# The second product of the last two blocks as seven products of sums (Strassen), in a sigmoid attention and MLP kernel on Trainium2

## The chip, the core and the metric

The kernel runs on one core of one Trainium2 chip. The metric is the device time of one execution in microseconds. The engines named below are TensorE (PE; PEld is its weight load), VectorE (DVE), ScalarE (ACT) and SyncE (SP), which only issues DMAs. GpSimd does nothing here.

## The reference

Sigmoid attention over 8 batches, 12 heads, 448 positions and head size 64, then an MLP of 768 -> 2048 -> 768 over all 3584 tokens, in float32:

```python
scores = scale * np.matmul(q, k.transpose(0, 1, 3, 2)) - np.log(S)
attn = 1.0 / (1.0 + np.exp(-scores))
x = np.matmul(attn, v)          # then tokens x 768
h = x @ w_in
g = h * (1.0 / (1.0 + np.exp(-1.702 * h)))
out = g @ w_out
```

## The kernel before

**Precision.** TensorE multiplies float32r. Every factor of a product that has to be exact is split in two parts, the rounded value and the rest; a product of two such factors is three matmuls: high by low, low by high, high by high. `round_and_rest` (L354) makes the parts: a cast (L357 on ScalarE or L358 on VectorE, whichever the plan finds free) and a subtraction on VectorE (L363).

**Blocks.** The 3584 tokens are 7 blocks of 512. Weights are 32 tiles of 128 x 768: 16 for w_in (f = 0 to 15) and 16 for w_out. They come as float64, are decoded, stored as float32 (`whole`), split, and stored as parts (`halves`, 128 x 1536: the rounded part, then the rest). From then on a block loads its weights from `halves` into the buffers `wsplit`, of which there are 3. The five blocks of `mlp` (L904) do the first layer ("up", 16 columns of 18 matmuls) and the second ("down", 6 columns of 48 matmuls).

**Attention** of later batches runs between the products of the blocks. Its batches 3 to 7 are `packed_attention` (L832): 60 units, one for a head of a pair, each of some scores (L717), sigmoids (L723), splits (L673, L765, L772) and a product with v (L806). Results are added into the blocks' x (L821); for blocks 3 to 5 x goes to HBM and back (`xd`).

**Order.** All instructions are put in an order beforehand by `Plan` (L78). It plays the tasks through with estimated costs; TensorE takes main units in their sequence and attention units as they fall due, the other engines take the ready task with the earliest key. `BUFS` says how many buffers each tag has; a new use of a buffer depends on all users of the use that many before it. `on_either` (L342) leaves ScalarE or VectorE to the plan. On the chip every engine runs its list in order, waiting on semaphores. All DMAs are issued by SyncE, in one list, so a DMA whose data isn't ready holds up all that are behind it.

**The last two blocks** (`last_blocks`, L987) are taken as one. Their x is a matrix of 2 x 2 quarters: two halves of the 768 inputs by two blocks (`one`, `two`). For the first layer, `up(n)` (L1059, n = 0 to 7) takes a pair of weight columns f, f2 (`columns`, L855) as a 2 x 2 matrix as well and makes the four results by seven products (Strassen's method in Winograd's form) rather than eight, 9 matmuls each (L1085). The factors of x (a11, a12 from x; s1 to s4 and a22 in the 15 buffers `xs`) are made once, by VectorE, after the attention has ended. Of the weights' sums (`sums_of_weights`, L858), there is one for each of the 8 column pairs: two loads of `whole`, four subtractions (L871), two splits, two stores (`sums`). They are tied to units 20, 25, ... 55 of the packed attention (L841).

The results h go through the sigmoid (L1047), the product with h (L1050) and `round_and_rest`, which makes the parts of g (`activated`, L1041), in 16 buffers `g`.

The second layer of the last two blocks (`down`, L1133) is plain: after every four `up` it adds up one half of the 16 rows of weights for all 6 output columns and both blocks: 2 halves x 6 x 2 x 8 x 3 = 576 matmuls (L1176). The first half's sums go to HBM (`od`) and come back (`osum`) to be added to the second's (L1004). A loaded buffer of weights holds 6 weight blocks, each used for both blocks, 36 matmuls.

Of the kernel before, what the change touches and what calls it, by code (L numbers as in the profile page):

```python
# [9 lines left out]
F32 = mybir.dt.float32  # L10
F32R = mybir.dt.float32r
# [9 lines left out]
P = 128  # L21
# [3 lines left out]
T = 512  # L25
# [230 lines left out]
def sigmoid_attention_mlp(ctx: ExitStack, tc: tile.TileContext, qk, v, v2, w, out):  # L256
# [575 lines left out]
    def packed_attention():  # L832
        units, late, n = [], [], 0
        for b in range(PACKED, B):
            for p in range(NP):
                loaded = load_pair(b, p)
                for j in range(2):
                    one, two, three = head(b, p, j, loaded)
                    units.append(one + two + late)
                    late = three  # L840
                    if len(units) > 18 and len(units) % 5 == 0 and n < NF // 2:  # L841
                        sums_of_weights(n, two)
                        n += 1
        assert n == NF // 2
        return [*units, late]

# [5 lines left out]
            for n in range(NF // 2)]  # L852
    summed = {}

    def columns(n):  # L855
        return 8 * (n // 4) + n % 4, 8 * (n // 4) + n % 4 + 4

    def sums_of_weights(n, after):  # L858
# [7 lines left out]
        h0, h1 = slice(0, HW), slice(HW, 2 * HW)  # L866

        def less(i, a, b, deps, first=lambda: None):
            def emit():
                first()  # L870
                nc.vector.tensor_tensor(t.tile[:, i * HW : (i + 1) * HW], a(), b(), op=ALU.subtract)  # L871

            return task("DVE", 0.55, emit, deps, [t, wa, wb])

        def of(i):
            return lambda: t.tile[:, i * HW : (i + 1) * HW]

        t1 = less(0, lambda: wb.tile[:, h0], lambda: wa.tile[:, h0], loads,
                  lambda: make(t, "raw64", [P, 2 * NW_EL], F32, f"sums{n}"))
        t2 = less(1, lambda: wb.tile[:, h1], of(0), [t1])  # L880
        t3 = less(2, lambda: wb.tile[:, h1], lambda: wb.tile[:, h0], [t1])
        t4 = less(3, lambda: wa.tile[:, h1], of(1), [t2])
# [104 lines left out]
    def last_blocks():  # L987
# [19 lines left out]

        for i in range(NK // 2):
# [11 lines left out]
            in_parts("a22", i, lambda b=a22: b.tile, wrote[two, i + NK // 2], [a22])  # L1020
            t1 = combine(lambda b=s1: b.tile, lambda b=a21: b.tile, lambda b=a22: b.tile, ALU.add, ready,
                         [s1, a21, a22], lambda b=s1, i=i: make(b, "line", [P, T], F32, f"s1_{i}"))
            in_parts("s1", i, lambda b=s1: b.tile, [t1], [s1])
            t2 = combine(lambda b=s2: b.tile, lambda b=s1: b.tile, lambda b=a11: b.tile, ALU.subtract,
                         [t1, l11], [s2, s1, a11], lambda b=s2, i=i: make(b, "line", [P, T], F32, f"s2_{i}"))
            in_parts("s2", i, lambda b=s2: b.tile, [t2], [s2])
            t3 = combine(lambda b=a21: b.tile, lambda b=a11: b.tile, lambda b=a21: b.tile, ALU.subtract,
                         [t1, l11], [a21, a11])
            in_parts("s3", i, lambda b=a21: b.tile, [t3], [a21])
            t4 = combine(lambda b=a12: b.tile, lambda b=a12: b.tile, lambda b=s2: b.tile, ALU.subtract,  # L1030
                         [t2, l12], [a12, s2])
            in_parts("s4", i, lambda b=a12: b.tile, [t4], [a12])

        units, gs = [], {}

# [5 lines left out]
        def activated(block, f, h, t, uses):  # L1041

            g, gb = buffer("line"), buffer("g")

            def sigmoid():
                make(g, "line", [P, T], F32, f"g{block}_{f}")
                nc.scalar.activation(g.tile, h(), AF.Sigmoid, scale=1.702)  # L1047

            t = task("ACT", 0.6, sigmoid, [t], [g, *uses])
            t = task("DVE", 0.69, lambda: nc.vector.tensor_tensor(g.tile, h(), g.tile, op=ALU.mult),  # L1050
                     [t], [g, *uses])
            t = round_and_rest(
                (0.62, 0.42, 0.69), gb, lambda: g.tile, [t], [g],
                lambda: gb.tile[:, 0], lambda: gb.tile[:, 1],
                lambda: make(gb, "g", [P, 2, T], F32R, f"gs{block}_{f}"),
            )
            gs[block, f] = (t, gb)
# [73 lines left out]
        halved = {}  # L1131

        def down(half):  # L1133

            fs = [8 * half + f for f in range(8)]
            blocks = [m * NF + f for m in range(NM) for f in fs]
            loaded, at = [], {}
            for n in range(0, len(blocks), NK):
                b = buffer("wsplit")
                ts, c = [], 0  # L1140
                for src, run in itertools.groupby(blocks[n : n + NK], lambda x: x // NK):
                    run = list(run)
                    while run:
                        count = next((i for i in range(1, len(run)) if run[i] != run[0] + i), len(run))
                        k, c0 = run[0] % NK, c
                        ts.append(dma(
                            lambda b=b, c0=c0, count=count: b.tile.bitcast(F32).rearrange(
                                "p (t c) -> p t c", t=2)[:, :, c0 * P : (c0 + count) * P],
                            lambda src=src, k=k, count=count: halves[NF + src].rearrange(
                                "p (t c) -> p t c", t=2)[:, :, k * P : (k + count) * P],  # L1150
                            2 * KB * count / NK, [saved[NF + src]], [b],
                            lambda b=b, n=n: b.tile is None and make(
                                b, "wsplit", [P, 2 * NW_EL], F32R, f"wd{half}_{n}"),
                        ))
                        for i in range(count):
                            at[run[i]] = (b, c0 + i, ts[-1])
                        run, c = run[count:], c + count
            turns = [(0, 1), (2, 4), (5, 6), (3, 7)]
            for m in range(NM):
                groups = []  # L1160
                for j, block in enumerate((one, two)):
                    bank = "m" if j == 0 else ("m0", "av")[m % 2]
                    groups.append((block, bank, buffer(bank)))
                steps = [(turn, g) for turn in turns for g in groups]
                if half and m == NM - 1:
                    steps = [(turn, g) for g in groups for turn in turns]
                for turn, (block, bank, ps) in steps:
                    pairs = [(at[m * NF + fs[i]], gs[block, fs[i]]) for i in turn]

                    def emit(pairs=pairs, ps=ps, bank=bank, turn=turn, block=block, m=m):  # L1170
                        if ps.tile is None:
                            make(ps, bank, [P, 512], F32, f"o{block}_{m}_{half}")
                        for i, ((b, c, _), (_, gb)) in zip(turn, pairs):
                            ws = [b.tile[:, j * NW_EL + c * P : j * NW_EL + (c + 1) * P] for j in range(2)]
                            for j, (u, d) in enumerate(((0, 1), (1, 0), (0, 0))):
                                nc.tensor.matmul(  # L1176
                                    ps.tile, lhsT=ws[u], rhs=gb.tile[:, d],
                                    start=i == 0 and j == 0, stop=i == 7 and j == 2,
                                )

                    t = task("PE", 6 * 0.2267, emit,
                             [d for x, g in pairs for d in (x[2], g[0])],
                             [ps, *(x[0] for x, _ in pairs), *(g[1] for _, g in pairs)])
                    units.append([t])
                    if turn != turns[-1]:
                        continue
                    if half == 0:
                        o = buffer("line")
                        t = on_either(
                            (0.59, lambda o=o, ps=ps: nc.scalar.copy(o.tile, ps.tile)),  # L1190
                            (0.69, lambda o=o, ps=ps: nc.vector.tensor_copy(o.tile, ps.tile)),
                            [t], [o, ps],
                            lambda o=o, block=block, m=m: make(o, "line", [P, T], F32, f"half{block}_{m}"),
                        )
                        d = dram.tile([P, T], F32, name=f"od{block}_{m}", tag=f"od{block}_{m}")
                        halved[block, m] = d, dma(
                            lambda d=d: d, lambda o=o: o.tile, P * T * 4 / 1024, [t], [o])
                    else:
                        d, t_d = halved[block, m]
                        o = buffer("x32")  # L1200
                        t_o = dma(lambda o=o: o.tile, lambda d=d: d, P * T * 4 / 1024, [t_d], [o],
                                  lambda o=o, block=block, m=m: make(o, "x32", [P, T], F32, f"osum{block}_{m}"))
                        t = combine(lambda o=o: o.tile, lambda ps=ps: ps.tile, lambda o=o: o.tile, ALU.add,
                                    [t, t_o], [o, ps])
                        dma(lambda block=block, m=m: out[block, m], lambda o=o: o.tile,
                            P * T * 4 / 1024, [t], [o])
# [69 lines left out]
```

## Time and profile before

| what | value |
|---|---|
| median of 3 runs | 1193.51 us (1192.75 to 1194.01) |
| the profiled execution | 1193.79 us |
| its span, first to last instruction | 1191.9 us |
| granted TensorE clock | 1.00 |
| TensorE busy | 1185.0 us, 5517 matmuls |
| VectorE busy | 873.0 us |
| ScalarE busy | 718.5 us |
| last matmul of the attention | 917 us |
| first layer of the last two blocks | 943.2 to 1000.3 and 1065.6 to 1122.7 us |
| their second layer | 1000.3 to 1065.6 and 1122.7 to 1188.0 us |

A row of the groups reads: line, engine, operation, output <- inputs by the program's names, shapes, count | busy us, mean ns of one | idle time of the engine just before them and what ended it. A row of the stages reads: stretch, then for each engine its busy us and its count, then the clock, the share of the 16 DMA engines, and GB/s. A row of the chain or the timeline reads: start, length, engine, line, what, count.

### The profile page before, as it was taken

To read this page: it belongs to the slowest core of one execution; us is meant where nothing else is said; L and a number is where in the kernel's file an instruction comes from. 1 tells how busy PE (TensorE), PEld (TensorE's weight loads), DVE (VectorE), ACT (ScalarE), POOL (GpSimd) and SP (SyncE) were. 2 spreads that over 40 slices of the span, in tenths; PEclk is the share of its full clock that TensorE was granted. 3 is DMA by queue.
4 is the path that set the end of the run, shared out by engine and by line. 5 is a ranking of instruction groups with operands and counts; after the bars stand their busy time and mean duration, and the time that the engine had idled before them with its cause. 6 is when DMAs were issued, how large, how long until landed. Compare 5 with 4: busy or idle time off the path is not lost.

```text
span 1191.9 us, 15238 instructions
## 1 busy us (share of the span) xinstructions
PE 1185.0 (99%) x5517; PEld 955.2 (80%) x5517; DVE 873.0 (73%) x1443; ACT 718.5 (60%) x1127; POOL 0.2 (0%) x4
## 2 busy tenths in 40 slices
PE   9999999999999999999999999999999999999998
PEld 4457777788888888888888888888888888888887
DVE  6989998769998598998789998588896464006511
ACT  7898887466787577786577786477784233013300
POOL 0000000000000000000000000000000000000000
PEclk9999999999999999999999999999999999999999
DMA  9966568867777655867766677757565755446652
GB/s 345 312 194 230 186 223 291 263 222 281 265 268 244 242 189 193 293 209 292 260 231 240 219 283 249 270 193 270 198 242 189 258 189 168 148 159 211 204 194 79
DMA packets 82154, 274.08 MB, mean 230 GB/s; under 512 B 8640, under 2 KB 15808, under 8 KB 82080
## 3 DMA queue, kind: packets, MB, share of 16 engines
q1 hardware_dynamic: 82080, 273.12, 66.9%
q8 instruction: 43, 0.70, 0.2%
q14 instruction: 31, 0.25, 0.1%
HBM read 203.88 MB, written 69.21 MB: 229 GB/s over the span
## 4 chain that ended last, share of the span: by engine, by line
PE 96%; DMA 2%; DVE 1%; ACT 1%; issue 0%; SPq 0%; ACTq 0%
PE h L912 28%; PE o L912 25%; PE o L1176 11%; PE sc L717 7%; PE av L806 7%; PE m L1085 5%; PE av L557 5%; PE sc L534 4%; PE sc L1085 3%; PE av L1085 1%; DMA wsplit<-w 1%; DMA wsum<-f 1%; DMA qkraw<-qk 0%; ACT a L545 0%; DVE qk L673 0%; DVE alo L772 0%
## 5 line engine op out<-in xcount | busy, mean ns | idle before, releaser
L912 PE MATMUL o<-gs,wsplit 128*128 128x512 f32 x1440 | 334.2, 390 | 0.6 <-DMA wsplit<-w 0.5
L912 PE MATMUL h<-x,wsplit 128*128 128x512 f32 x1440 | 334.1, 390 | 0.0
L912 PEld LDWEIGHTS o<-gs,wsplit 128*128 128x128 f32 x1440 | 269.9, 188 | 58.2 <-DMA wsplit<-w 1.5
L912 PEld LDWEIGHTS h<-x,wsplit 128*128 128x128 f32 x1440 | 269.9, 188 | 56.9 <-issue 1.3
L1176 PE MATMUL o<-gs,wd 128*128 128x512 f32 x576 | 130.9, 389 | 0.0
L1176 PEld LDWEIGHTS o<-gs,wd 128*128 128x128 f32 x576 | 108.1, 188 | 22.5
L723 ACT ACTIVATE a<-sc,bias 128x448 f32<-128x448 f32 x120 | 98.3, 820 | 33.5 <-PE sc L717 26.4
L673 DVE TENSOR_TENSOR qk<-qkraw,qk 64x64 fp32r<-64x64 f32 x180 | 111.5, 619 | 5.4 <-ACT qk L678 0.7
L357 ACT CAST gs<-g 128x512 fp32r<-128x512 f32 x109 | 67.7, 621 | 76.4 <-DVE g L944 55.9
L772 DVE TENSOR_TENSOR alo<-a,ahi 128x448 fp32r<-128x448 f32 x120 | 101.3, 847 | 3.5 <-ACT ahi L765 2.4
L717 PE MATMUL sc<-qk 128*128 128x448 f32 x420 | 94.9, 365 | 0.0
L717 PEld LDWEIGHTS sc<-qk 128*128 128x128 f32 x420 | 78.9, 188 | 9.1
L1004 DVE TENSOR_TENSOR h<-h,m 128x512 f32<-128x512 f32 x28 | 19.2, 686 | 86.7 <-PE m L1085 86.7
L363 DVE TENSOR_TENSOR gs<-g,gs 128x512 fp32r<-128x512 f32 x112 | 76.7, 687 | 8.1 <-ACT gs L357 6.5
L765 ACT CAST ahi<-a 128x448 fp32r<-128x448 f32 (+2 forms) x124 | 80.3, 666 | 2.1
L545 ACT ACTIVATE a<-sc,bias 112x896 f32<-112x896 f32 x72 | 68.8, 1005 | 15.0 <-PE sc L534 8.6
L748 DVE COPY rest<-sc 64x448 f32<-64x448 f32 x48 | 30.1, 626 | 65.0 <-ACT a L723 60.8
L806 PE MATMUL av<-ahi,v 128*128 128x448 f32 x240 | 58.4, 365 | 0.0
L557 PE MATMUL av<-a,vraw 112*64 112x448 f32 x288 | 57.9, 545 | 0.0
L939 ACT ACTIVATE g<-h 128x512 f32<-128x512 f32 x80 | 47.6, 596 | 16.9 <-PE h L912 15.8
L944 DVE TENSOR_TENSOR g<-h,g 128x512 f32<-128x512 f32 x80 | 55.0, 688 | 1.6 <-ACT g L939 0.3
L363 DVE TENSOR_TENSOR wsplit<-wraw,wsplit 128x768 fp32r<-128x768 f32 x48 | 45.7, 952 | 12.1 <-ACT wsplit L357 11.8
(102 smaller groups left out, 1336.0 us busy)
## 6 DMA issues: line engine op xcount, KB each, us to landing
wsplit<-w SPq DMA_DIRECT2D x96, 768.0 KB, 5.1
w<-w SPq DMA_DIRECT2D x40, 768.0 KB, 5.2
w<-wsplit SPq DMA_DIRECT2D x32, 768.0 KB, 5.7
qkraw<-qk SPq DMA_DIRECT2D x48, 448.0 KB, 4.0
wraw<-f SPq DMA_DIRECT2D x48, 384.0 KB, 4.2
f<-w SPq DMA_DIRECT2D x32, 384.0 KB, 4.8
t<-tsplit SPq DMA_DIRECT2D x16, 768.0 KB, 6.2
w<-t SPq DMA_DIRECT2D x16, 768.0 KB, 4.6
```

What stands on the lines that cost most here:

```text
L363: lambda: nc.vector.tensor_tensor(lo(), src(), hi().bitcast(F32), op=ALU.subtract),
L545: nc.scalar.activation(a.tile[:C, c % 2], ps.tile[:C, :, :S], AF.Sigmoid, bias=bias[:C], scale=scale)
L557: nc.tensor.matmul(ps.tile[cols, :S], lhsT=vr.tile[:C, j, c], rhs=a.tile[:C, c % 2, j], start=c == 0, stop=c == NC - 1,)
L673: return lambda: nc.vector.tensor_tensor(s.tile[rows, into], qkr.tile[own, cols], s.tile[own, cols].bitcast(F32), op=ALU.subtract)
L717: nc.tensor.matmul(out, lhsT=s.tile[:, cols], rhs=s.tile[:, r : r + S], start=n == 0, stop=n == len(terms) - 1,)
L723: nc.scalar.activation(out, x, AF.Sigmoid, bias=bias[:rows], scale=scale)
L765: (costs[0], lambda: nc.scalar.copy(hi_at(), cols())),
L772: nc.vector.tensor_tensor(lo_at(), cols(), hi_at().bitcast(F32), op=ALU.subtract)
L806: nc.tensor.matmul(av.tile[:, :S], lhsT=vs.tile[:, c].rearrange("p a d -> p (a d)"), rhs=m, start=n == 0, stop=n == len(todo) - 1,)
L912: nc.tensor.matmul(ps, lhsT=ws[a], rhs=x[:, c], start=first and i == 0, stop=last and i == 2)
L1085: nc.tensor.matmul(ps, lhsT=ws[c], rhs=x[:, d], start=not more and i == 0 and j == 0, stop=i == NK // 2 - 1 and j == 2, skip_group_check=more,
L1176: nc.tensor.matmul(ps.tile, lhsT=ws[u], rhs=gb.tile[:, d], start=i == 0 and j == 0, stop=i == 7 and j == 2,)
```

## The change

All 8 `up` come first, then one `down`. It takes the 2048 x 1024 matrix g (two blocks of 512 tokens) and w_out as 2 x 2 quarters, even rows of weights against odd ones and the first three output columns against the last three, and makes the result by seven products, named a11, a12, a22, s1, s2, s3, s4 by their factor of g. Each is 3 columns x 8 rows x 3 passes = 72 matmuls. Results are added in VectorE, or by going on in the same bank of PSUM (a12 after a11, s4 after s1).

- g stays in float32 in its 16 buffers (`activated` no longer rounds). `combine_all` makes s1, s2, s3, s4 in place, and `parts_of` splits one factor after another into the 15 buffers `xs`, which now serve the first layer's factors and then the 56 parts of g.
- The 15 parts of x are split in another order: s2, s3, s1, a22, s4, each for its three rows.
- `sums_of_weights` runs 16 times instead of 8, for the pairs of w_in as before and for the pairs of w_out; it is tied to units 12, 15, ... 57.
- A buffer `wsplit` of the second layer is filled by two loads of 384 KB and serves 18 matmuls. For a11, a12 and s4 a load takes every other 128 columns of `halves`, in pieces of 512 B; for the other four it takes 1536 B pieces of `sums`.
- The halves of the output no longer go to HBM and back.

```diff
-                    if len(units) > 18 and len(units) % 5 == 0 and n < NF // 2:
+                    if len(units) > 10 and len(units) % 3 == 0 and n < NW // 2:
                         sums_of_weights(n, two)
...
     def columns(n):
-        return 8 * (n // 4) + n % 4, 8 * (n // 4) + n % 4 + 4
+        if n < NF // 2:
+            return 8 * (n // 4) + n % 4, 8 * (n // 4) + n % 4 + 4
+        return NF // 2 + n, NW // 2 + n
...
+        for name in ("s2", "s3", "s1", "a22", "s4"):
+            for i in range(NK // 2):
+                b, deps = todo[i][name]
+                in_parts(name, i, lambda b=b: b.tile, deps, [b])
...
         def activated(block, f, h, t, uses):
-            g, gb = buffer("line"), buffer("g")
+            g, gb = buffer("line"), gbs[f]
...
-            t = round_and_rest(
-                (0.62, 0.42, 0.69), gb, lambda: g.tile, [t], [g],
...
+            gs[block, f] = task("DVE", 0.69, times, [t], [g, gb, *uses])
...
+            parts_of("a11", a11, lambda i: [gs[one, 2 * i]])
+            parts_of("a12", a12, lambda i: [gs[one, 2 * i + 1]])
+            parts_of("a22", a22, lambda i: [gs[two, 2 * i + 1]])
+            s1 = combine_all(a22, a21, a22, ALU.add, lambda i: [gs[two, 2 * i], got["a22"][i]])
+            parts_of("s1", a22, lambda i: [s1[i]])
+            s2 = combine_all(a22, a22, a11, ALU.subtract, lambda i: [gs[one, 2 * i], got["s1"][i]])
+            parts_of("s2", a22, lambda i: [s2[i]])
+            s3 = combine_all(a21, a11, a21, ALU.subtract, lambda i: [gs[one, 2 * i], s1[i]])
+            parts_of("s3", a21, lambda i: [s3[i]])
+            s4 = combine_all(a12, a12, a22, ALU.subtract, lambda i: [s2[i], got["a12"][i]])
+            parts_of("s4", a12, lambda i: [s4[i]])
...
+                        def src(f=f, j=j):
+                            return halves[f].rearrange("p (t i two c) -> p two t i c", t=2, two=2, c=P)[:, j]
...
+            def products(name, banks, bufs, more):
+                ends, ws = [], weights(name)
+                for m in range(NM // 2):
+                    ps, bank = bufs[m], banks[m]
+                    for part in range(4):
...
+            three, other = ("sc", "sc", "av"), ("m0", "m", "m")
...
+            p1 = products("a11", three, ps, [])
+            u = copies("x32", "p1", three, ps, p1)
+            p2 = products("a12", three, ps, [t for _, t in u])
...
-        for half in range(2):
-            for n in range(4):
-                up(4 * half + n)
-            down(half)
+        for n in range(NF // 2):
+            up(n)
+        down()
```

The order of instructions, at three places. First TensorE where the second layer of block 2 begins its fourth column (`o_3`) and a unit of attention (`sc`, `av`) falls due. Before:

```order
L912 MATMUL o_2_5229<-gs_15_4957,wsplit_5222 128x512 x3
L912 MATMUL o_3_5355<-gs_0_4140,wsplit_5259 128x512 x3
L912 MATMUL o_3_5355<-gs_1_4211,wsplit_5259 128x512 x3
L717 MATMUL sc_1_0_0_5370<-qk_1_0_5199 128x448 x3
L717 MATMUL sc_1_0_1_5378<-qk_1_0_5199 128x448 x4
L806 MATMUL av_0_1_5387<-alo_0_1_5314,v_0_1_5146 128x448 x3
L806 MATMUL av_0_1_5387<-ahi_0_1_5302,v_0_1_5146 128x448 x4
L912 MATMUL o_3_5355<-gs_2_4244,wsplit_5259 128x512 x3
```

After:

```order
L920 MATMUL o_2_5292<-gs_15_4982,wsplit_5284 128x512 x3
L717 MATMUL sc_1_0_0_5417<-qk_1_0_5267 128x448 x3
L717 MATMUL sc_1_0_1_5425<-qk_1_0_5267 128x448 x4
L806 MATMUL av_0_1_5435<-alo_0_1_5359,v_0_1_5203 128x448 x3
L806 MATMUL av_0_1_5435<-ahi_0_1_5353,v_0_1_5203 128x448 x4
L920 MATMUL o_3_5454<-gs_0_4161,wsplit_5324 128x512 x3
L920 MATMUL o_3_5454<-gs_1_4235,wsplit_5324 128x512 x3
L920 MATMUL o_3_5454<-gs_2_4270,wsplit_5324 128x512 x3
```

Here the unit of attention stands one pair of products earlier. Nine units move like this, earlier or later; all else on TensorE is in the old order up to the last two blocks' second layer.

Second VectorE where the new sum of weights at unit 15 (`sums`, `tsplit`) enters, beside the splits of a head (`qk`, `rest`) and the g of block 1 (`g`, `gs`). Before:

```order
L944 TENSOR_TENSOR g_2_4231<-h_2_4184,g_2_4231 128x512
L363 TENSOR_TENSOR gs_1_4211<-g_1_4155,gs_1_4211 128x512
L363 TENSOR_TENSOR gs_2_4244<-g_2_4231,gs_2_4244 128x512
L748 COPY rest_1_1_4268<-sc_1_1_0_4253 64x448
L944 TENSOR_TENSOR g_3_4257<-h_3_4223,g_3_4257 128x512
```

After:

```order
L952 TENSOR_TENSOR g_2_4256<-h_2_4207,g_2_4256 128x512
L882 TENSOR_TENSOR sums_4268<-wsum_4232,wsum_4200 128x384
L363 TENSOR_TENSOR gs_1_4235<-g_1_4176,gs_1_4235 128x512
L882 TENSOR_TENSOR sums_4268<-wsum_4232,sums_4268 128x384
L882 TENSOR_TENSOR sums_4268<-wsum_4232 128x384
L882 TENSOR_TENSOR sums_4268<-wsum_4200,sums_4268 128x384
L363 TENSOR_TENSOR gs_2_4270<-g_2_4256,gs_2_4270 128x512
L363 TENSOR_TENSOR tsplit_0_4281<-sums_4268,tsplit_0_4281 128x768
L363 TENSOR_TENSOR tsplit_1_4289<-sums_4268,tsplit_1_4289 128x768
L751 TENSOR_TENSOR rest_1_1_4309<-sc_1_1_0_4284,rest_1_1_4309 64x448
```

Six instructions of the sum stand ahead of the head's work, and the copy of its `rest` has gone to ScalarE.

Third TensorE at the seam between the first layer's last product and the second layer (`o` are results, `wd` the weights). Before, after the fourth `up`:

```order
L1085 MATMUL av_9355<-xs_2_8945,w_3_9195 128x512 x3
L1176 MATMUL o_0_0_9405<-gs_0_9026,wd_0_9350 128x512 x3
L1176 MATMUL o_0_0_9405<-gs_1_9135,wd_0_9350 128x512 x3
L1176 MATMUL o_0_0_9418<-gs_0_9088,wd_0_9350 128x512 x3
L1176 MATMUL o_0_0_9418<-gs_1_9197,wd_0_9350 128x512 x3
```

After, behind the eighth `up` (`ga` are the parts of a11; the trailing numbers of a name tell its row):

```order
L1096 MATMUL av_9868<-xs_2_9085,w_7_9718 128x512 x3
L1235 MATMUL oa_0_9934<-ga_0_9841,wda_0_9863 128x512 x3
L1235 MATMUL oa_0_9934<-ga_1_9844,wda_0_9863 128x512 x3
L1235 MATMUL oa_0_9934<-ga_2_9847,wda_0_9863 128x512 x3
L1235 MATMUL oa_0_9934<-ga_3_9878,wda_0_9863 128x512 x3
L1235 MATMUL oa_0_9934<-ga_4_9882,wda_0_9863 128x512 x3
L1235 MATMUL oa_0_9934<-ga_5_9885,wda_0_9863 128x512 x3
L1235 MATMUL oa_0_9934<-ga_6_9899,wda_2_9901 128x512 x3
```

A buffer of weights now serves six triples in a row, each with another part of g.

More of the change, by code (lines that the diff above doesn't have):

```diff
@@ L851, in sigmoid_attention_mlp, with row_half @@
     sums = [[dram.tile([P, 2 * NW_EL], F32, name=f"t{n}_{j}", tag=f"t{n}_{j}") for j in range(2)]
-            for n in range(NF // 2)]
+            for n in range(NW // 2)]
     summed = {}
     def columns(n):
-        return 8 * (n // 4) + n % 4, 8 * (n // 4) + n % 4 + 4
+        if n < NF // 2:
+            return 8 * (n // 4) + n % 4, 8 * (n // 4) + n % 4 + 4
+        return NF // 2 + n, NW // 2 + n
+    def row_half(t, n, j):
+        if n < NF // 2:
+            return t[:, j * HW : (j + 1) * HW].rearrange("p (i c) -> p i c", c=P)
+        return t.rearrange("p (i two c) -> p two i c", two=2, c=P)[:, j]
     def sums_of_weights(n, after):
@@ L865, in sums_of_weights, with of @@
         ]
-        h0, h1 = slice(0, HW), slice(HW, 2 * HW)
+        def of(i):
+            return lambda: t.tile[:, i * HW : (i + 1) * HW].rearrange("p (i c) -> p i c", c=P)
         def less(i, a, b, deps, first=lambda: None):
@@ L870, in emit @@
                 first()
-                nc.vector.tensor_tensor(t.tile[:, i * HW : (i + 1) * HW], a(), b(), op=ALU.subtract)
+                nc.vector.tensor_tensor(of(i)(), a(), b(), op=ALU.subtract)
             return task("DVE", 0.55, emit, deps, [t, wa, wb])
[L875 to L882, printed above, removed]
+        w11, w21, w12, w22 = (lambda b=b, j=j: row_half(b.tile, n, j) for b in (wa, wb) for j in range(2))
+        t1 = less(0, w12, w11, loads, lambda: make(t, "raw64", [P, 2 * NW_EL], F32, f"sums{n}"))
+        t2 = less(1, w22, of(0), [t1])
+        t3 = less(2, w22, w12, [t1])
+        t4 = less(3, w21, of(1), [t2])
         for j, deps in enumerate(([t1, t2], [t3, t4])):
@@ L1006, in combine @@
             return task("DVE", 0.69, emit, deps, uses)
+        todo = {}
         for i in range(NK // 2):
@@ L1047, in sigmoid, with times @@
                 nc.scalar.activation(g.tile, h(), AF.Sigmoid, scale=1.702)
+            def times():
+                if gb.tile is None:
+                    make(gb, "g", [P, 2, T], F32, f"gs{f}")
+                nc.vector.tensor_tensor(gb.tile[:, block - one], h(), g.tile, op=ALU.mult)
             t = task("ACT", 0.6, sigmoid, [t], [g, *uses])
-            t = task("DVE", 0.69, lambda: nc.vector.tensor_tensor(g.tile, h(), g.tile, op=ALU.mult),
-                     [t], [g, *uses])
-            t = round_and_rest(
-                (0.62, 0.42, 0.69), gb, lambda: g.tile, [t], [g],
[L1054 to L1057, printed above, removed]
+            gs[block, f] = task("DVE", 0.69, times, [t], [g, gb, *uses])
         def up(n):
@@ L1129, in up @@
             activated(one, f2, in12, c12, [h12])
[L1131 to L1197, printed above, removed]
-                    else:
[L1199 to L1206, printed above, removed]
```

117 lines of the change are left out of this document (111 added, 6 removed).

## The prediction

> **What bounds the kernel now.** I read the page's busy line and its chain first, to learn which engine sets the end.
>
> ```profile
> span 1191.9 us, 15238 instructions
> PE 1185.0 (99%) x5517; PEld 955.2 (80%) x5517; DVE 873.0 (73%) x1443; ACT 718.5 (60%) x1127; POOL 0.2 (0%) x4
> PE 96%; DMA 2%; DVE 1%; ACT 1%; issue 0%; SPq 0%; ACTq 0%
> ```
>
> TensorE is busy 99% of the span and is 96% of the chain. Work taken off it shortens the span, unless something else becomes late. Next the waits of TensorE, which tell what can still be late.
>
> ```profile
> PE still L319 <- DVE still L316: 1.5, 1, 1.5
> PE sc L534 <- DMA qkraw<-qk: 0.6, 1, 0.6
> PE o L912 <- DMA wsplit<-w: 0.5, 1, 0.5
> PE sc L534 <- ACT a L545: 0.2, 1, 0.2
> ```
>
> All of TensorE's waits add up to 2.8 us, and three of the four lie in the warm-up and the first attention (L319, L534). So there is almost no idle time to win, and any wait that the change makes is new. Then the busy time by stage: four equal pieces of the attention stage in which the change adds work, and the two second products of the last two blocks.
>
> ```profile
> core 0: us, PE busy (x) PEld busy (x) DVE busy (x) ACT busy (x) POOL busy (x), PEclk, DMA share, GB/s
> 375.00:500.00 125.00, 125.00 (x567) 106.06 (x566) 101.00 (x175) 86.13 (x142) 0.00 (x0) 1.00 0.65 225
> 500.00:625.00 125.00, 125.00 (x568) 106.15 (x567) 106.57 (x185) 84.46 (x144) 0.00 (x0) 1.00 0.72 252
> 625.00:750.00 125.00, 125.00 (x571) 106.85 (x570) 110.00 (x192) 93.17 (x156) 0.00 (x0) 1.00 0.73 253
> 750.00:875.00 125.00, 124.45 (x563) 105.17 (x562) 104.02 (x176) 86.66 (x145) 0.00 (x0) 1.00 0.67 235
> 1000.30:1065.60 65.30, 65.30 (x290) 54.07 (x289) 3.40 (x6) 8.36 (x15) 0.00 (x0) 1.00 0.45 145
> 1122.70:1188.10 65.40, 65.31 (x289) 53.74 (x287) 11.07 (x18) 1.89 (x4) 0.00 (x0) 1.00 0.44 145
> ```
>
> In the attention stage TensorE is full and VectorE is 81 to 88% full. In the two second products TensorE is full while VectorE and ScalarE have next to nothing to do and the DMA engines are under half used. The clock is 1.00 throughout. Last the end of the chain:
>
> ```profile
> 1120.69 2.04 PE av L1085 x9
> 1122.73 65.29 PE o L1176 x288
> 1188.05 0.69 DVE osum L1004
> ```
>
> The 288 matmuls of a half take 65.29 us without a gap, 0.2267 us each; the nine of a product of the first layer, 2.04 us, have the same price.
>
> **The change part by part.** (1) *Matmuls.* Before, the second product is 2 halves x 6 output columns x 2 blocks x 8 rows of weights x 3 passes = 576 matmuls. After, it is 7 products x 3 columns x 8 rows x 3 passes = 504, of the same shape. That takes away 72 x 0.2267 = 16.32 us of the engine that is the chain. [...]
>
> (2) *Eight more sums of weights, in the attention stage.* The prices:
>
> ```profile
> L871 DVE TENSOR_TENSOR sums<-wsum,sums 128x384 f32<-128x384 f32 x16 | 8.8, 550 | 0.0
> L363 DVE TENSOR_TENSOR tsplit<-sums,tsplit 128x768 fp32r<-128x768 f32 x16 | 15.0, 953 | 0.0
> L357 ACT CAST tsplit<-sums 128x768 fp32r<-128x768 f32 x16 | 13.4, 837 | 17.3 <-DVE sums L871 17.0
> ```
>
> One sum of weights costs VectorE 4 x 0.550 + 2 x 0.953 = 4.1 us and ScalarE 2 x 0.837 = 1.7 us; eight cost 33 and 13 us. They come every third unit of attention instead of every fifth, from the 12th unit on. The tightest quarter is 625 to 750; of L871 alone it holds
>
> ```profile
> 625.00:750.00 125.00, 4.55 (x9) 1.00 0.73 253
> ```
>
> nine subtractions, 2.25 sums. By the times of the units five will stand there: 110.0 + 2.75 x 4.1 = 121.3 of 125 us, 97%. So VectorE still has room, and the order moves only nine attention units on TensorE, most of them by one pair of products. The cover is this 3%. What happens where it is gone is seen in the one wait of this stage:
>
> ```profile
> 762.35 0.70 DVE L821 TENSOR_TENSOR x<-av,tmp 64x384 f32<-64x384 f32 x2
> 762.93 0.32 SPq L338 DMA_DIRECT2D xd<-x  x1
> 763.35 0.40 SPq L338 DMA_DIRECT2D wsplit<-w  x1
> ...
> 769.15 1.21 PE L912 MATMUL o<-gs,wsplit 128*128 128x512 f32 x4 [0.55 <-DMA wsplit<-w]
> ```
>
> SyncE issues in order. Its store of x waits for VectorE, the load of weights stands behind it, and TensorE waits 0.55 us for those weights. A sum of weights was being made just before. The eight sums of before thus go with 0.55 us of waits; eight more I put at as much again, 0.55 us. The ends: below nothing by those 0.55 us, if this wait goes since the order shifts; above, 8 x 4.1 = 33 us, if nothing of the added VectorE time is hidden. I take a value near the low end, because the eight sums that run already cost so little beside a VectorE that is just as full. The added DMAs of a sum, two loads of 384 KB and two stores of 768 KB, bring 18.9 MB into some 500 us, 38 GB/s on top of about 240; DMA shares of 0.65 to 0.73 leave that room.
>
> (3) *The first layer of the last two blocks* loses the rounding of g (32 casts, 32 subtractions), which is off the chain: its products run back to back. The reordering of the parts of x only sets which of the 15 slots comes free first. Cost 0.
>
> (4) *The seam.* Before, two seams stood between layers; now there is one, and the parts of g must wait for slots which the parts of x hold. The last first-layer step frees three slots each after its 2nd, 4th, 5th, 6th and 7th product. The parts of the first factor need the first eight, free 18 matmuls (4.1 us) before the seam at the latest, and the last two are used 18 matmuls after it: 8.2 us for a cast and a subtraction of 1.3 us. No wait.
>
> (5) *VectorE and ScalarE in the seven products:*
>
> ```profile
> L363 DVE TENSOR_TENSOR gs<-g,gs 128x512 fp32r<-128x512 f32 x112 | 76.7, 687 | 8.1 <-ACT gs L357 6.5
> L357 ACT CAST gs<-g 128x512 fp32r<-128x512 f32 x109 | 67.7, 621 | 76.4 <-DVE g L944 55.9 <-DVE g L1050 20.0
> L1004 DVE TENSOR_TENSOR osum<-o,osum 128x512 f32<-128x512 f32 x12 | 8.3, 692 | 53.3 <-PE o L1176 53.3
> L1190 ACT COPY half<-o 128x512 f32<-128x512 f32 x12 | 7.1, 588 | 55.5 <-PE o L1176 55.5
> ```
>
> 56 subtractions, 32 sums of factors and 15 additions of results at 0.69 us are 71 us of VectorE in 504 x 0.2267 = 114.3 us; 48 casts and 11 copies are 36 us of ScalarE. Of the eight parts of a factor, seven take slots of the factor two products back, a whole product (16.3 us) ahead; the eighth takes the first slot of the product just before, free after 54 of its 72 matmuls, and is read 21 matmuls into the next: 39 x 0.2267 = 8.8 us for about 2 us of work. Cost 0.
>
> (6) *Weights.* A buffer now serves 18 matmuls, 4.08 us, not 36, and is filled by two loads of 384 KB. Three buffers give 8.2 us from a buffer's release to its next use. For three of the seven products (a11, a12, s4) the rows of a load are pieces of 512 B, a size that no load of before has; the smallest are 1024 B. Two stretches of one microsecond, the first with 1024 B pieces, the second with 6144 B ones:
>
> ```profile
> DMA packets 375, 0.36 MB, mean 360 GB/s; under 512 B 24, under 2 KB 375, under 8 KB 375
> q1 hardware_dynamic: 375, 0.36, 105.6%
> ...
> DMA packets 65, 0.37 MB, mean 375 GB/s; under 512 B 4, under 2 KB 4, under 8 KB 65
> q1 hardware_dynamic: 65, 0.37, 91.4%
> ```
>
> With 16 engines a piece of 1024 B takes 16 x 1.056 / 351 = 48 ns and one of 6144 B 16 x 0.914 / 61 = 240 ns, a line of 37 ns per KB plus 10 ns. That puts 512 B at an estimated 29 ns, so a load (48 pieces an engine) at 1.4 us and a buffer at 2.8 us of 4.08. The bound from above is that a piece of 512 B takes as long as one of 1024 B: 2 x 48 x 0.048 = 4.6 us, 0.54 us over in each of 12 buffers, 6.5 us. I take 0, since the line lies far under 4.08 and hardly any fixed share shows.
>
> (7) *The end.* As before one addition and one store follow the last matmul. Cost 0.
>
> The sum, on the profiled execution (1193.79 us, which is the span and 1.9 us around it): 1193.79 - 16.32 + 0.55 = 1178.0. That execution is 0.3 above the median of 1193.51, so the forecast is **1177.7 us**.
>
> **The rivals.**
> A, *short rows bind.* At 4.6 us a buffer the three products with 512 B pieces take up to 6.5 us more: 1177.7 + 6.5 = 1184.2. For it: no such piece is in the trace. Against: the line above. It costs from 42 ns a piece (4.08 / 96). Chance 0.10.
> B, *some of the added VectorE work shows.* If each new sum costs 1 us through the SyncE queue as at 762 us, eight cost 8 us: 1185. For it: 97% in the tightest quarter. Against: 0.55 us for eight sums so far. Chance 0.12.
> C, *slower: VectorE becomes the bound of the attention stage.* More than half of the 33 us must show, over 2 us a sum; with all of it, 1177.2 + 33 = 1210. It would need several more quarters like 625 to 750 to pass 100%; none comes there by the count. Chance 0.03.
> D, *loads in single file.* 56 loads of 384 KB replace 32 larger or equal pieces. If each had to land before the next began, at the landing time of such a load below, a buffer took 8.4 us and 28 buffers 28 x 4.3 = 121 us more, slower by far.
>
> ```profile
> wraw<-f SPq DMA_DIRECT2D x48, 384.0 KB, 4.2
> ...
> 1114.60 7.95 SPq L338 DMA_DIRECT2D wd<-w  x7
> ```
>
> Seven loads go out within 7.95 us and the engines are full at 1024 B pieces, so loads overlap. [...] Chance 0.02.
> E, *nothing gained*: new waits in the seven products eat the 16 us (1193). The leads of 8 us in (4) to (6) speak against it. Chance 0.02.
>
> **How the numbers follow.** The forecast has 0.71: 1177.7, with 1176.5 if the wait at 769 us goes too and the tail is a little shorter, and 1180 with a few waits as long as that one. The range goes on through A to its bound and most of B: 1176.5 to 1184.2. That leaves out C, D, E and a little of B, under 2 in 10. A difference of 0.2%, 2.4 us, is about what a measurement of this kernel can tell from none. Faster: 0.71 + 0.10 + 0.12 = 0.93; same 0.02 (E); slower 0.05 (C, D).
>
> **What would show it.** In the changed kernel: 5445 matmuls; the new second product as one piece of 504 matmuls and some 114.3 us with no wait of TensorE; waits of TensorE in the attention stage of about 1 us in all; VectorE at 97% between 625 and 750 us. Wrong would be: waits for weights of a11, a12 or s4 (A), a row of waits for weights behind SyncE's stores between 380 and 900 us (B, C), or waits for parts of g (E).

## The result, and the profile after

The changed kernel took 1178.38 us (median of 4 runs, 1177.34 to 1179.68) beside 1193.70 us (median of 4, 1192.75 to 1194.01) for the kernel before: a ratio of 0.9874, with a 95% interval of 0.9856 to 0.9891. The profiled execution took 1177.94 us; the sum of the prediction for a profiled execution was 1178.0.

The page's span, busy line and chain of the changed kernel:

```profile
span 1176.2 us, 15372 instructions
PE 1168.7 (99%) x5445; PEld 941.9 (80%) x5445; DVE 936.8 (80%) x1551; ACT 744.0 (63%) x1166; POOL 0.2 (0%) x4
PE 92%; DVE 3%; ACT 2%; DMA 2%; issue 0%; DVEq 0%; SPq 0%; ACTq 0%
```

TensorE has lost 72 matmuls and 16.3 us of busy time (1185.0 to 1168.7) and is still 99% busy. VectorE has gained 63.8 us and ScalarE 25.5 us, while TensorE stayed full. The waits of TensorE (total, times, longest):

```profile
PE still L319 <- DVE still L316: 1.5, 1, 1.5
PE sc L534 <- DMA qkraw<-qk: 0.9, 1, 0.9
PE av L806 <- DVE alo L772: 0.5, 1, 0.5
PE sc L717 <- ACT a L723: 0.4, 1, 0.4
PE sc L534 <- ACT a L545: 0.3, 1, 0.3
```

The wait for weights behind SyncE's store, 0.5 us before, is gone. Two new ones of 0.4 and 0.5 us stand in the attention (L717, L806), both at one place, shown below. None stands in the last two blocks. By stage (PE, PEld, DVE, ACT, POOL busy, clock, DMA share, GB/s), and last the subtractions of the sums of weights alone:

```profile
500.00:625.00 125.00, 124.05 (x562) 104.95 (x561) 109.12 (x189) 88.53 (x149) 0.00 (x0) 1.00 0.81 285
625.00:750.00 125.00, 125.00 (x570) 106.77 (x569) 117.90 (x207) 93.73 (x158) 0.00 (x0) 1.00 0.79 283
750.00:875.00 125.00, 125.00 (x567) 106.15 (x567) 110.54 (x185) 89.87 (x150) 0.00 (x0) 1.00 0.77 267
1057.00:1172.00 115.00, 115.00 (x509) 95.19 (x507) 64.79 (x109) 29.96 (x50) 0.00 (x0) 1.00 0.69 207
...
625.00:750.00 125.00, 8.39 (x16) 1.00 0.79 283
```

Between 625 and 750 us VectorE went from 110.0 to 117.9 us, 94%; the prediction said 121.3, 97%. Sixteen subtractions, four sums, stand there, not five. In the second product of the last two blocks VectorE has work for 56% of the time, and TensorE doesn't wait for it. The end of the chain:

```profile
1056.05 2.04 PE av L1096 x9
1058.09 48.96 PE oa L1235 x216
1107.05 65.29 PE os L1235 x288
```

The last product of the first layer ends at 1058.09 and the first of the second begins there. The 504 matmuls take 48.96 + 65.29 = 114.25 us without a gap; the 576 of before took 65.30 + 65.29. That is -16.34. All that lies ahead of the seam took 0.66 us more than before (1058.09 us, and 1188.02 - 130.59 = 1057.43).

**The one new wait.** It is read from the chain around it:

```profile
556.95 1.10 DVE alo L772
558.07 5.04 DMA wsum<-f
563.13 0.57 DVE sums L882
...
568.75 1.02 ACT a L723
569.79 0.64 DVE ahi L766
570.45 1.10 DVE alo L772
...
571.60 1.48 PE av L806 x6
```

and from SyncE's and VectorE's rows at the same place, with SyncE's last wait between 553 and 560 us ahead of them:

```profile
SPq L338 <- DVE alo L772: 0.9, 1, 0.9
...
556.73 0.32 SPq L338 DMA_DIRECT2D xd<-x  x1
558.07 0.32 SPq L338 DMA_DIRECT2D wsum<-f  x1
...
563.13 0.56 DVE L882 TENSOR_TENSOR sums<-wsum,wsum 128x384 f32<-128x384 f32 x1 [2.92 <-DMA wsum<-f]
```

It is a circle. SyncE's store of x (`xd`) waits for VectorE until 556.73, and the load of the second tile of a sum stands behind it in SyncE's list. That load then waits 0.9 us more on its own account, until VectorE has ended a split of the attention (`alo`, 556.95 + 1.10); a sum's tiles and the inputs of these splits share the buffers `w32`. It lands 5 us later; VectorE, in order, waits 2.92 us for it; the attention's splits behind it come late, and TensorE with them. In the circle of the prediction's step (2) a late store held back TensorE's weights. Here the wait that ended last is the load's own, for VectorE, and the circle closes over VectorE.

No run took the circle apart, but the eight profiled executions with these 16 sums (the changed kernel twice, E1, E3, E4, E6, E9 and E10) bear it out. Where VectorE waited 1.24 to 2.39 us for this load (five executions), TensorE did not wait there. At 2.92, 4.00 and 4.43 us it waited 0.95, 2.41 and 2.44 us. So the same stretch of work costs TensorE nothing or a few microseconds, depending on the execution.

### The profile page after: what moved, and what is told of

The parts are those of the page before. It is cut to its first block, busy times and chain, and to the rows that moved or that the text cites. A ratio compares the mean times of both kernels' runs of the same rounds, so it can differ in the third digit from the quotient of the medians.

```text
span 1176.2 us, 15372 instructions
## 1 busy us (share of the span) xinstructions
PE 1168.7 (99%) x5445; PEld 941.9 (80%) x5445; DVE 936.8 (80%) x1551; ACT 744.0 (63%) x1166; POOL 0.2 (0%) x4
## 4 chain that ended last, share of the span: by engine, by line
PE 92%; DVE 3%; ACT 2%; DMA 2%; issue 0%; DVEq 0%; SPq 0%; ACTq 0%
PE h L920 27%; PE o L920 24%; PE av L806 6%; PE sc L717 6%; PE os L1235 6%; PE m L1096 6%; PE av L557 5%; PE sc L534 4%; PE oa L1235 4%; PE sc L1096 3%; PE av L1096 1%; DMA wsum<-f 1%; ACT a L723 1%; DMA x<-xd 1%; DMA xd<-x 0%; DVE alo L772 0%
## 5 line engine op out<-in xcount | busy, mean ns | idle before, releaser
L772 DVE TENSOR_TENSOR alo<-a,ahi 128x448 fp32r<-128x448 f32 x120 | 100.8, 848 | 3.5 <-ACT ahi L765 2.4
L717 PE MATMUL sc<-qk 128*128 128x448 f32 x420 | 95.2, 366 | 0.4 <-ACT a L723 0.4
L765 ACT CAST ahi<-a 128x448 fp32r<-128x448 f32 (+2 forms) x132 | 85.6, 671 | 3.1 <-DMA t<-tsplit 1.1
L717 PEld LDWEIGHTS sc<-qk 128*128 128x128 f32 x420 | 78.8, 188 | 9.9 <-ACT a L723 0.8
L357 ACT CAST gs<-g 128x512 fp32r<-128x512 f32 x75 | 46.5, 620 | 50.1 <-DVE g L952 49.6
L1235 PE MATMUL os<-gs,wds 128*128 128x512 f32 x288 | 65.4, 389 | 0.0
L1235 PEld LDWEIGHTS os<-gs,wds 128*128 128x128 f32 x288 | 54.1, 188 | 11.2
L806 PE MATMUL av<-ahi,v 128*128 128x448 f32 x240 | 58.4, 365 | 0.0
L363 DVE TENSOR_TENSOR gs<-g,gs 128x512 fp32r<-128x512 f32 x80 | 54.3, 685 | 4.7 <-ACT gs L357 4.1
L748 DVE COPY rest<-sc 64x448 f32<-64x448 f32 x44 | 27.5, 625 | 36.0 <-ACT a L723 31.8
L947 ACT ACTIVATE g<-h 128x512 f32<-128x512 f32 x80 | 47.6, 595 | 12.8 <-PE h L920 12.0
L723 ACT ACTIVATE a<-rest,bias 64x448 f32<-64x448 f32 x60 | 40.1, 669 | 21.0 <-DVE rest L751 20.7
```

The lines of the kernel that those rows point to most:

```text
L363: lambda: nc.vector.tensor_tensor(lo(), src(), hi().bitcast(F32), op=ALU.subtract),
L717: nc.tensor.matmul(out, lhsT=s.tile[:, cols], rhs=s.tile[:, r : r + S], start=n == 0, stop=n == len(terms) - 1,)
L723: nc.scalar.activation(out, x, AF.Sigmoid, bias=bias[:rows], scale=scale)
L765: (costs[0], lambda: nc.scalar.copy(hi_at(), cols())),
L772: nc.vector.tensor_tensor(lo_at(), cols(), hi_at().bitcast(F32), op=ALU.subtract)
L806: nc.tensor.matmul(av.tile[:, :S], lhsT=vs.tile[:, c].rearrange("p a d -> p (a d)"), rhs=m, start=n == 0, stop=n == len(todo) - 1,)
```

## The experiments

The theory: the second product is worth its 72 matmuls, because the added sums of weights, the loads in short rows and the work on g's factors all lie beside TensorE. The rivals are those of the prediction: A (short rows), B and C (the sums of weights show), E (new waits in the seven products). The medians are of 4 to 11 runs, and those of the kernel before of 7 to 15.

**E1, the sum of weights alone.** The kernel before, with all of the change to `sums_of_weights`, whose eight new sums nobody reads:

```diff
-                    if len(units) > 18 and len(units) % 5 == 0 and n < NF // 2:
+                    if len(units) > 10 and len(units) % 3 == 0 and n < NW // 2:
                         sums_of_weights(n, two)
...
```

> The kernel before with the change's 16 sums of weights at units 12, 15, ... 57, and nothing else of the change (the eight new sums are stored and not read). Theory: the added VectorE work is hidden but for a wait or two, so 0 to 1.5 us over the kernel before, about 1194.2 us, with TensorE's waits between 375 and 943 us at 0.6 to 2 us. Rival (the added VectorE work shows, 1 us a sum or more): 1201 us or above.

Measured: 1192.52 us (1192.15 to 1196.63) beside 1193.17; ratio 0.9999 (0.9990 to 1.0008). Its stage from 625 to 750:

```profile
625.00:750.00 125.00, 125.00 (x570) 106.83 (x569) 117.93 (x207) 94.26 (x158) 0.00 (x0) 1.00 0.79 284
```

VectorE is as full as in the changed kernel, and TensorE is busy throughout; its only waits, 2.3 us in all, are three in the warm-up and the first attention (L319, L534). The 0.6 to 2 us of waits that were expected after 375 us did not come. Eight more sums cost nothing in the median, within 1 us.

**E2, the change without the added sums.** The changed kernel with the eight sums of before; the second layer reads sums of w_in for those of w_out.

```diff
-                    if len(units) > 10 and len(units) % 3 == 0 and n < NW // 2:
+                    if len(units) > 18 and len(units) % 5 == 0 and n < NF // 2:
...
-                        deps = [summed[n, k // 2]]
+                        deps = [summed[i, k // 2]]
...
```

> The changed kernel with only the eight sums of before at their old places; the four products that want sums of w_out load those of w_in in their place, so the sizes and the loads stay and the output is not the reference's. Theory: the matmuls alone, 1193.7 - 16.3 = 1177.4 us, 0 to 1.5 us under the changed kernel's 1178.4. Rival (the sums cost 1 us each and the second layer gains more than its matmuls): 1170 us.

Measured: 1176.86 us (1175.92 to 1177.63), ratio 0.9863 (0.9850 to 0.9877). This lay 1.5 us under the changed kernel's 1178.38, which came from other runs, so both were run again on one chip:

> The changed kernel as it is, once more, on the same chip as the kernels beside it. Theory (the added sums of weights are hidden, so the kernels with and without them differ by no more than the waits): 1176.5 to 1178.5 us, within 1 us of the kernel without the added sums. Rival (the added sums cost something that the profile shows as scattered waits, some 1.5 us): 1.2 to 2.5 us over the kernel without them.

> The changed kernel with only the eight old sums of weights, at their old places; the second layer loads the sums of w_in where it would load those of w_out, so its output isn't the reference's. Theory: 1176.5 to 1177.5 us, within 1 us of the changed kernel. Rival (the added sums cost some 1.5 us): 1.2 to 2.5 us below the changed kernel.

Measured: the changed kernel 1176.67 us (1175.34 to 1176.92), ratio 0.9863 (0.9846 to 0.9879); without the added sums 1177.16 us (1175.75 to 1177.55). So the 1.5 us were not the sums. In this execution of the changed kernel VectorE waited 2.39 us for the load of the circle, and TensorE didn't wait there at all.

**E3 and E4, other rows of weights.** In the loads for a11, a12 and s4 the pieces become 1536 B, or 256 B, of the same tiles and as many bytes, so that the columns are the wrong ones.

```diff
-                            return halves[f].rearrange("p (t i two c) -> p two t i c", t=2, two=2, c=P)[:, j]
+                            return halves[f].rearrange("p (t two i c) -> p two t i c", t=2, two=2, c=P)[:, j]
```

```diff
-                            return halves[f].rearrange("p (t i two c) -> p two t i c", t=2, two=2, c=P)[:, j]
+                            return halves[f].rearrange("p (t i two c) -> p two t i c", t=2, two=2, c=P // 2)[:, j]
...
-                        return t.rearrange("p (t i c) -> p t i c", t=2, c=P)
+                        return t.rearrange("p (t i c) -> p t i c", t=2, c=P // 2 if name in ("a11", "a12", "s4") else P)
```

> The changed kernel with the loads of a11, a12 and s4 in pieces of 1536 B (three neighbouring column blocks) in place of 512 B; the weights are the wrong ones, their number and size the same. Theory: 512 B pieces are fast enough (an estimated 29 ns against 42 ns allowed), so the same time within 1 us, and no wait of TensorE for these loads in either. Rival (short pieces bind): up to 6 us faster.

> The changed kernel with the loads of a11, a12 and s4 in pieces of 256 B, half the size and twice the number (wrong weights, same bytes). If the line through 1024 and 6144 B (10 ns and 37 ns per KB) goes on, a piece takes 19 ns, a buffer 3.7 us of the 4.08 that it serves: the same time, up to 2 us more. If a piece can't be faster than the 29 ns put down for 512 B, a buffer takes 5.6 us and the twelve buffers cost about 18 us: 1196 us, with TensorE waiting for weights in a11, a12 and s4.

Measured: 1536 B 1177.09 us (1175.21 to 1180.94), 0.9870 (0.9852 to 0.9887); 256 B 1176.39 us (1176.32 to 1177.60), 0.9858 (0.9844 to 0.9873). The longest run with 1536 B, 1180.94 us, is the profiled one. It lost its time ahead of the seam, which came at 1061.09: TensorE waited 2.44 us at the place of the circle, and behind that the clock was at 0.50 from 572 to 574 us. The end of the chain with 256 B pieces:

```profile
1056.56 48.96 PE oa L1235 x216
1105.52 65.29 PE os L1235 x288
```

No gap, at half the size of the change's pieces. Rival A is out. The pieces do cost the DMA engines something. From 1040 to 1105 us the queue moved 12.69, 13.08 and 12.95 MB with pieces of 512, 256 and 1536 B, and its packets took 65.7, 80.5 and 61.3% of the 16 engines' time. The median time of these loads from issue to landing, in the same order:

```profile
wda<-w SPq DMA_DIRECT2D x16, 384.0 KB, 4.5
```

```profile
wda<-w SPq DMA_DIRECT2D x16, 384.0 KB, 5.3
```

```profile
wda<-w SPq DMA_DIRECT2D x16, 384.0 KB, 4.0
```

They land 0.5 us and 1.3 us later than long rows, and neither has an effect on the time here: the first of the loads is issued 8.13 us before the seam with each size (1049.96 for 1058.09, 1048.43 for 1056.56, 1052.96 for 1061.09), and the 504 matmuls behind the seam have no gap.

**E5, 24 sums.** The changed kernel with eight sums more, which nobody reads, every second unit:

```diff
-                    if len(units) > 10 and len(units) % 3 == 0 and n < NW // 2:
+                    if len(units) > 10 and len(units) % 2 == 0 and n < NW // 2 + 8:
...
```

> The changed kernel with eight sums of weights more than it needs (24, one behind every second unit from the 12th on; the last eight are stored and not read). VectorE would stand at 117.9 + 8.2 = 126 of 125 us between 625 and 750 us and at 94% in the other quarters. Theory (a sum costs nothing until VectorE is full): 1 to 5 us more, from waits in that quarter, 1181 us. Rival (each sum costs a little through SyncE's list, VectorE full or not): as much again as the first eight, 1179 us. Rival (VectorE binds at once): 1190 us or more.

Measured: 1188.52 us (1187.90 to 1190.30), ratio 0.9959 (0.9945 to 0.9974), 10 to 12 us over the changed kernel. That is twice and more what the theory had (1 to 5 us), and close under the rival by which VectorE binds at once (1190 us). The step from eight sums to sixteen costs nothing; the step from sixteen to 24 costs a third of the 33 us added. The waits that are new, and the tightest quarter:

```profile
PE av L806 <- DVE alo L772: 3.7, 8, 0.6
PE sc L717 <- ACT a L723: 2.0, 2, 1.8
...
625.00:750.00 125.00, 121.15 (x528) 100.46 (x528) 117.76 (x205) 97.47 (x164) 0.00 (x0) 0.97 0.84 299
```

VectorE is no busier than in the changed kernel there (117.8 us, where 126 were expected), which fits a TensorE, and with it an attention feeding VectorE, that has become slower. To learn which half of a sum costs this, arithmetic or transfers, each was added alone.

**E11 and E12, the transfers alone, the arithmetic alone.** At 24 places every third one takes, instead of a sum, only its loads and stores, or only its arithmetic on a constant.

```diff
+                    if len(units) > 10 and len(units) % 2 == 0 and n < 24:
+                        if n % 3 == 2:
+                            extra(n, two)
+                        else:
+                            sums_of_weights(n - (n + 1) // 3, two)
...
```

> The changed kernel plus, eight times between its sums of weights (24 places, every second unit from the 12th, each third one extra), the transfers of a sum alone: two loads of 384 KB and stores of 1536 KB that nobody reads, with no work on VectorE or ScalarE. The kernel with 24 whole sums took 10 to 12 us more than the changed kernel. Theory V (VectorE is full and the added arithmetic shows): 0 to 2 us over the changed kernel (1176.7 to 1178.4). Theory S (the circle from VectorE through SyncE's list and the buffers that a sum holds, back to VectorE): 5 to 12 us over.

> The changed kernel plus, at the same eight places, the arithmetic of a sum alone on a buffer filled with a constant: one fill, four subtractions, two casts and two subtractions of the low part, some 4.5 us of VectorE, with no transfers; nobody reads it. Theory V (VectorE is full): 5 to 12 us over the changed kernel, with waits of TensorE for the attention's splits between 600 and 720 us. Theory S (the transfers and what waits behind them): 0 to 2 us over.

Measured: transfers 1180.91 us (1180.10 to 1184.28), ratio 0.9908 (0.9895 to 0.9922), 2.5 to 4.2 us over the changed kernel (by the ratios, each beside its own runs of the kernel before, 4 to 5), more than the 0 to 2 of theory V and at the lower end or below the 5 to 12 of theory S. Arithmetic 1189.44 us (1188.50 to 1191.34), ratio 0.9974 (0.9963 to 0.9985), 11.1 to 12.8 us over. The largest new wait with the transfers, then two with the arithmetic, two of its quarters, and the 10 us that lead up to one of these waits (at 710 us):

```profile
PE h L934 <- DMA wsplit<-w: 1.6, 2, 1.3
```

```profile
PE av L806 <- DVE alo L772: 3.8, 7, 0.9
PE av L806 <- DVE ahi L772: 1.3, 2, 1.0
...
500.00:625.00 125.00, 120.01 (x533) 98.88 (x532) 112.84 (x196) 92.00 (x156) 0.00 (x0) 1.00 0.77 275
625.00:750.00 125.00, 123.13 (x555) 102.99 (x553) 119.90 (x207) 100.03 (x169) 0.00 (x0) 1.00 0.73 264
...
700.00:710.00 10.00, 9.24 (x44) 7.47 (x42) 9.73 (x18) 9.70 (x19) 0.00 (x0) 1.00 0.96 375
```

The arithmetic alone costs as much as whole sums do; with its fills and casts it is some 40 us of VectorE, beside 33 for eight sums. It also holds buffers of the attention's splits (`w32`, `raw64`, `a`), so the time alone can't tell VectorE's work from its buffers. The rows can, in part: TensorE waits for a split of VectorE (L772) at eight places, and in the 10 us that lead up to the wait VectorE is 96 to 98% busy at six of them, with hardly a gap between its instructions. There its list is behind. At the other two it is 92 and 80% busy; in the stretch of 80% it had itself waited 1.77 us for the load of a sum. So the reserve that was nearly used up is mostly VectorE's. By quarters, 90 and 96%, it would still seem to have room. The changed kernel has stretches as full (98% from 690 to 710 us) and TensorE doesn't wait behind them: there a full stretch alone did no harm.

The arithmetic's profile also has a wait of 1.6 us for weights (`wsplit`). Transfers alone cost a quarter to two fifths as much, in their profile mainly through late weights (new waits of 1.6 us, beside 0.7 for VectorE's splits); the two costs don't add up to that of whole sums.

**E6, the old order of x's parts.**

```diff
-        for name in ("s2", "s3", "s1", "a22", "s4"):
-            for i in range(NK // 2):
+        for i in range(NK // 2):
+            for name in ("a22", "s1", "s2", "s3", "s4"):
```

> The changed kernel with the 15 parts of x split in the old order (a22, s1, s2, s3, s4 for each row). Theory: the order only sets which slot comes free first, and the worst part (a11's fifth, whose slot is free at the seam) is used 2.7 us after it: 0 to 0.5 us. Rival (the seam lives from the new order): a wait of 2 to 4 us of TensorE at the seam, 1181 us.

Measured: 1176.24 us (1176.16 to 1177.59), ratio 0.9861 (0.9848 to 0.9875), with no wait at the seam. The order of the parts is worth nothing here.

**E9, the low parts of g's factors made twice.**

```diff
+                again = task(
+                    "DVE", 0.69,
+                    lambda: nc.vector.tensor_tensor(x.tile[:, 1], at(), x.tile[:, 0].bitcast(F32), op=ALU.subtract),
+                    [parts["g" + name, i][0]], [x, b],
+                )
...
```

> The changed kernel, with each of the 56 subtractions that make the low part of g's factors done twice, with the same result. VectorE gets 56 x 0.69 = 38.6 us more in the second product, 71 + 39 = 110 of 114.3 us, 96%. Theory (the leads of 16.3 and 8.8 us take up what stands uneven, and VectorE binds only when its work does not fit): the same time as the changed kernel to 4 us over it. Rival (the cover in the second product is thin, as rival E had it: work in VectorE shows there at once): half of the added work or more, 19 to 39 us over. A third way, by the kernel with 24 sums, where VectorE was full at 94 to 98% and each short wait cost TensorE about 1 us: 4 to 12 us over.

Measured: 1177.60 us (1176.89 to 1178.58), ratio 0.9870 (0.9856 to 0.9885), 0.9 us over the changed kernel beside it. The stage of the second product:

```profile
1057.00:1172.00 115.00, 115.00 (x509) 95.05 (x507) 94.74 (x156) 34.41 (x58) 0.00 (x0) 1.00 0.67 207
```

VectorE goes from 64.8 to 94.7 us, 82% (eight casts more are ScalarE's), and TensorE stays full. The 96% that was expected was not reached, so the test says nothing on the last 20 us. The 0.9 us, no more than the spread of the runs, lie outside this stage as far as the profiled execution shows. Rival E is out, with some 30 us of VectorE to spare.

**E10, six products.** The changed kernel without its last product, s4:

```diff
-            parts_of("s4", a12, lambda i: [s4[i]])
...
-            for m, t in enumerate(products("s4", three, keep, [t for _, t in c22])):
...
+            for m in range(up_to):
+                store(one, m + up_to, *u[m])
```

> The changed kernel without its seventh product, s4: neither its 72 matmuls nor its factor, weights and three additions are made, so a quarter of the output isn't the reference's. Theory (TensorE alone sets the length of the second product): 72 x 0.2267 = 16.3 us less than the changed kernel, 15.8 to 16.8. Rival (the products are near another bound, loads or VectorE, which takes over as matmuls go): less than 14 us less.

Measured: 1162.45 us (1161.46 to 1164.19), ratio 0.9744 (0.9729 to 0.9760): 14.2 us less than the changed kernel beside it. That is 1.6 us short of what the theory expected and just over the bound of the rival. The seam of the changed kernel in that session, then the end of the chain with six products:

```profile
1055.50 48.96 PE oa L1235 x216
...
1056.48 48.96 PE oa L1233 x216
1105.44 48.97 PE os L1233 x216
...
1154.44 0.70 DVE u L1012
...
1155.16 0.69 DVE p L1012
```

The product is worth its 16.32 us (97.93 for 114.25). In the two profiled executions 0.98 us come back ahead of the seam (1056.48 for 1055.50), no more than executions of one kernel differ there (1055.50 and 1058.09 for the changed kernel), and 1.4 us behind the last matmul, where now two additions stand in a row and more is left to store (5.3 us to the span's end for 3.9). So -16.32 + 0.98 + 1.4 = -13.9, as the two executions show (1161.46 and 1175.34). The expectation had left out the tail.

## Why the prediction was right, point by point

1. *Matmuls, -16.32.* Held: -16.34 in the rows, at 226.7 ns a matmul as before (114.25 us for 504), and again -16.32 for the next 72 in E10.
2. *Eight more sums, +0.55 of 33.* Held in size, but not by the wait that it was put together from. Measured: 0 within 1 us in the medians (E1; E7 beside E8), and in the result's profiled execution 0.95 us of new waits, with the old one of 0.5 us gone. The step took the old wait for weights to go with the sums, and put eight more at as much again. But waits for weights don't follow the number of sums: with 16, E1 has none and E4 one of 1.0 us; with eight, E8 has one of 0.3 us. What came was another wait, over VectorE, in some executions and not in others. Two more things in the step were off. It counted five sums into the tightest quarter, where four stand: 110.0 + 1.75 x 4.1 = 117.2 would have met the 117.9 measured. And it took the room for what is left to 100% of a quarter. E12 shows waits for VectorE's list with 90% and 96% in two quarters, so the change ended closer to the edge than the step said; the edge lies between 16 and 24 sums.
3. *First layer, 0.* Held: 114.24 us for 114.22; E6 shows that the order of x's parts doesn't matter either way.
4. *Seam, no wait.* Held: 1056.05 + 2.04 = 1058.09, where the next row begins.
5. *VectorE and ScalarE beside the seven products, 0.* Held, with room (E9).
6. *Short rows, 0.* Held, down to 256 B (E4). The bound of 6.5 us, from the price of a 1024 B piece, was far from it.
7. *The end, 0.* Held: one addition and one store, as before.

The rivals: A fell to E4, B to E1 and E8. C did not come at eight added sums; E12 shows its mechanism at eight more, at 11 to 13 us of some 40 us of work, still short of its price. D and E are out by the 504 matmuls without a gap. The forecast of 1177.7 us lies between the two medians of the changed kernel, 1176.67 and 1178.38.

That 1178.0 met 1177.94 to a tenth is luck. In another execution of the same kernel the seam came 2.6 us earlier (1055.50 for 1058.09), more than any term of the sum but the first. What the record shows is the first term, to 0.02 us.

## What to carry to other kernels

Where one engine is the whole chain and full, its instructions taken away are worth their full price, here 16.3 us for 72 matmuls, less what then shows at the ends (1.4 us in E10); the question is which list falls behind as its cover shrinks. Look for the reserve of the helpers in short stretches, and not in the average of a long one: in E12 a quarter of 125 us at 90% held 10 us at 97.5%, behind which TensorE waited. A doubtful cover is tested by adding work to the helper until it shows, arithmetic and transfers apart.

## What the runs showed that was not expected

**A short wait costs TensorE more than its row says.** Two attention products in E5, the first with a wait, the second without:

```profile
618.85 0.36 PE L806 MATMUL av<-alo,v 128*128 128x448 f32 x1
619.85 0.68 PE L806 MATMUL av<-alo,v 128*128 128x448 f32 x2 [0.63 <-DVE alo L772]
620.50 1.08 PE L806 MATMUL av<-ahi,v 128*128 128x448 f32 x4
621.41 8.34 PE L921 MATMUL h<-x,wsplit 128*128 128x512 f32 x36
...
666.12 0.77 PE L806 MATMUL av<-alo,v 128*128 128x448 f32 x3
666.73 0.97 PE L806 MATMUL av<-ahi,v 128*128 128x448 f32 x4
667.54 8.35 PE L921 MATMUL h<-x,wsplit 128*128 128x512 f32 x36
```

The seven matmuls take 621.41 - 618.85 = 2.56 us with a recorded wait of 0.63, and 1.42 without: the wait costs 1.14 us, at a clock of 1.00 in both places. Back to back the rows overlap (0.77 and 0.97 us lie in 1.42); around the wait they overlap less, both ahead of it and behind it. Why, the rows don't show. With the clock below, it may be part of why E5's recorded waits grew by 5.9 us (9.5 for 3.6) and its time by 10 to 12.

**The clock halved behind waits of 1.81 and 0.51 us, but not behind 1.91 and 0.50.** E5's longest wait, and rows of the time after it, from 712 to 720 us:

```profile
709.91 1.08 PE L717 MATMUL sc<-qk 128*128 128x448 f32 x4 [1.81 <-ACT a L723]
...
712.00:714.00 2.00, 2.00 (x6) 1.78 (x6) 1.97 (x5) 1.76 (x3) 0.00 (x0) 0.50 0.67 136
...
716.00:718.00 2.00, 2.00 (x7) 1.53 (x6) 1.96 (x3) 1.98 (x4) 0.00 (x0) 0.52 0.70 276
718.00:720.00 2.00, 2.00 (x10) 1.63 (x9) 1.97 (x5) 1.97 (x4) 0.00 (x0) 1.00 0.54 162
```

For about 6 us TensorE ran at half clock, by an estimate from these rows some 3 us lost. In E6 a wait of 1.91 us, with one of 0.50 us behind it, left the clock at 1.00 (from 565 to 575 us). So waits of nearly the same length ended differently, and no run here shows why.
